# Centring the first four tiles before their transposes, and starting five FFN blocks tile by tile instead of three

## The chip, the cores and the metric

The kernel runs on one core of a Trainium2 chip. That core has a matrix engine (TensorE, PE in the profile), a vector engine (VectorE, DVE), a scalar engine (ScalarE, ACT), a general engine (GpSimd, POOL) and a sync engine (SyncE, SP) that here only issues transfers. Each works through its own list of instructions in order, and waits where an instruction needs something from another engine. The metric is the device time of one execution in microseconds (us), taken as the median of several runs.

## What is computed

The input `x` has 2048 rows (tokens) of 640 columns. Everything is in bfloat16, with sums in float32.

```
xn  = layernorm(x)                         # per row: (x - mean) / sqrt(var + 1e-5)
q, k, v = xn @ wqkv                        # 32 heads of 20 columns
phi(t) = where(t > 0, t + 1, exp(t)) + 1e-6
kv  = phi(k)^T v     per head;   z = sum over tokens of phi(k)
s   = (phi(q) kv) / (phi(q) z + 1e-6) @ wo
g   = silu(relu(xn @ w1) @ w2)             # FFN, 1728 hidden columns
out = x + s * g
```

The attention is linear: `kv` and `z` are sums over all tokens, so all of K must be known before any output row is. The FFN does not depend on the attention.

## The kernel before

The tokens are cut into 16 tiles of 128 and four groups of 512 (group j holds tiles 4j to 4j+3). Matrix products need the normalized input transposed, with the 640 columns as five chunks of 128 on the partitions; this is `xnT`. Three kinds of work use it:

- a *K block* (`K_mm`, L468) takes one tile through the K weights, 2 x 5 matmuls of 128x320;
- an *FFN block* (`H_block`, L565) takes 128 of the 1728 hidden columns for a whole group, 5 matmuls of 128x512, and ScalarE's relu then empties the PSUM bank (`H_ev`);
- a *Q block* (`Q_block`) does the same for the queries of groups 1 to 3 (those of group 0 come later).

After them come the Gram blocks `G_block` for `kv`, the FFN's second product `U_main`, and the output tiles `s_tile`. There is no planner. The order in which the calls stand in the source is the order of each engine's list, and a small bookkeeping class (`Sched`) adds the waits: an operation that reads or overwrites something waits for whoever wrote or still reads it. The PSUM banks (eight of them, `ps[0]` to `ps[7]`) are given by hand.

The first group is special, since nothing is transposed when the kernel starts. While TensorE runs filler matmuls (`fill`), the first tile is loaded, its mean and variance are found by VectorE (`LN_stats`: two statistics and one aggregate), the mean is subtracted in two parts, and the parts are transposed by TensorE (`T_first`). Tiles 1 to 3 are transposed raw (`T_raw`), copied out of PSUM, and the mean is removed afterwards: TensorE sums the 640 columns with a matrix of ones (`T_sum`, L450), and VectorE subtracts the result in place (`T_center`, L455). The division by the standard deviation is not done here for these four tiles; the readers of K and the final silu apply it as a scale. As soon as a tile is ready, the first three FFN blocks are computed for that tile alone (`H_first`, 128 columns wide), in banks 2, 3 and 4. When all four tiles are done, ScalarE empties these banks, and the list `order` (L684) goes on with K blocks of tiles 0 to 7 (`K_step`) and the FFN blocks 3 to 12 of group 0 between them. Tiles 4 to 7 are normalized by VectorE in that time (`LN_norm`, L407) and transposed by a DMA (`xnT_dma`, L463).

The transfers are issued by SP in the order of the source, each some 0.4 us after the one before; an `extra` entry holds a transfer back until a given operation is done. Only the first part of `w1` (FFN blocks 0 to 2) goes out on ScalarE's queue. `w1` is cut into three parts at the limits `W1C`; a block waits for its part alone.

Of the kernel before, what the change touches and what calls it, by code (L numbers as in the profile page):

```python
# [4 lines left out]
ALU = mybir.AluOpType  # L5
# [206 lines left out]
def bass_recurrent_scan__linear_attn_block__dense_activation_relu__prompt_kernel(  # L212
# [14 lines left out]
    P = 128  # L227
# [73 lines left out]
    mhalf = nc.alloc_sbuf_tensor("mhalf", [P, 1], f32)  # L301
    denS = nc.alloc_sbuf_tensor("denS", [P, 512], f32)
    rden = nc.alloc_sbuf_tensor("rden", [P, 512], bf)
    stats = nc.alloc_sbuf_tensor("stats", [P, T, 2, 6], f32)
    mv = nc.alloc_sbuf_tensor("mv", [P, T, 2], f32)
    rsv = nc.alloc_sbuf_tensor("rsv", [P, T], f32)
# [26 lines left out]
    def x_load(t, extra=(), E="SP"):  # L333
        sl = t % XR
        return dma(E, lambda eng: eng.dma_start(xin[:, sl, :], x2[tok(t), :]), W=[("xin", sl)], extra=extra)
# [8 lines left out]
    sc.op("POOL", lambda eng: eng.memset(ident[:], 0.0), W=[("ident",)])  # L344
    sc.op("POOL", lambda eng: eng.affine_select(out=ident[:], in_=ident[:], compare_op=ALU.not_equal,
                                                fill=1.0, base=0, pattern=[[-1, P]], channel_multiplier=1),
          R=[("ident",)], W=[("ident",)])
# [7 lines left out]
                        for _ in range(n)], W=[("ps", 0)])  # L355


    W1C = [0, 3 * P, 7 * P, FF]

    def w1_load(i, extra=()):  # L360
        w_load(w1_sb[:, :, W1C[i]:W1C[i + 1]], B_w1[:, W1C[i]:W1C[i + 1]], ("w1", i), extra)

    def w1_part(f):
        return [i for i in range(3) if W1C[i] <= P * f < W1C[i + 1]][0]

    x_load(0)
    for t in (1, 2, 3):
        x_load(t)
    dma("ACT", lambda eng: eng.dma_start(w1_sb[:, :, W1C[0]:W1C[1]],
                                         B_w1[:, W1C[0]:W1C[1]].rearrange("(c p) n -> p c n", p=P)), W=[("w1", 0)])  # L370

    def build_masks():
        sc.op("POOL", lambda eng: eng.memset(mh[:, :, :], 1.0), W=[("mh",)])
# [29 lines left out]
    def xnk(t, cs=range(C)):  # L403
        return [("xn", t, c) for c in cs]
# [6 lines left out]
            x_load(t + XR)  # L411


    def T_first(c0, c1):
        done = sc.op("DVE", lambda eng: eng.tensor_scalar(
            out=xn[:, 0, P * c0:P * c1], in0=xin[:, 0, P * c0:P * c1], scalar1=mv[:, 0, 0:1], scalar2=None,
            op0=ALU.subtract), R=[("xin", 0), ("mv", 0)], W=xnk(0, range(c0, c1)))
        b = 4 if c0 == 0 else 1
        psb = ps[b].bitcast(bf)
        sc.group("PE", [(lambda eng, c=c: eng.transpose(psb[:, P * c:P * (c + 1)], xn[:, 0, P * c:P * (c + 1)], ident[:]))  # L420
                        for c in range(c0, c1)], R=xnk(0, range(c0, c1)) + [("ident",)], W=[("ps", b)])
        out = xnT[:, c0:c1, 0:P]
        src = psb[:, P * c0:P * c1].rearrange("p (c q) -> p c q", c=c1 - c0)
        if c0 == 0:
            sc.op("ACT", lambda eng: eng.activation(out=out, in_=src, func=ACTF.Copy), R=[("ps", b)],
                  W=xtk(0, range(c0, c1)))
        else:
            sc.op("DVE", lambda eng: eng.tensor_copy(out, src), R=[("ps", b)], W=xtk(0, range(c0, c1)))
        return done


    def T_raw(t):
        psb = ps[4 + t].bitcast(bf)
        cut = 3 if t == 1 else C
        psc = ps[0].bitcast(bf)
        for c0, c1, pd, pb in [(0, cut, psb, 4 + t), (cut, C, psc, 0)]:
            if c1 > c0:
                sc.group("PE", [(lambda eng, c=c, pd=pd: eng.transpose(pd[:, P * c:P * (c + 1)],
                                                                       xin[:, t, P * c:P * (c + 1)], ident[:]))
                                for c in range(c0, c1)], R=[("xin", t), ("ident",)], W=[("ps", pb)])  # L440
        sc.op("ACT", lambda eng: eng.activation(out=xnT[:, 0:cut, tok(t)],
                                                in_=psb[:, 0:cut * P].rearrange("p (c q) -> p c q", c=cut),
                                                func=ACTF.Copy), R=[("ps", 4 + t)], W=xtk(t, range(cut)))
        if cut < C:
            sc.op("DVE", lambda eng: eng.tensor_copy(xnT[:, cut:C, tok(t)],
                                                     psc[:, cut * P:C * P].rearrange("p (c q) -> p c q", c=C - cut)),
                  R=[("ps", 0)], W=xtk(t, range(cut, C)))

    def T_sum(t):
        sc.group("PE", [(lambda eng, c=c: eng.matmul(ps[4 + t][:, 320:320 + P], lhsT=onesM[:, :], rhs=xnT[:, c, tok(t)],  # L450
                                                     start=(c == 0), stop=(c == C - 1))) for c in range(C)],
                 R=xtk(t) + [("onesM",)], W=[("ps", 4 + t)])

    def T_center(t):
        return sc.op("DVE", lambda eng: eng.scalar_tensor_tensor(  # L455
            out=xnT[:, :, tok(t)], in0=ps[4 + t][:, 320:320 + P].unsqueeze(1).to_broadcast([P, C, P]), scalar=-1.0 / D,
            in1=xnT[:, :, tok(t)], op0=ALU.mult, op1=ALU.add), R=[("ps", 4 + t)] + xtk(t), W=xtk(t))

    def xtk(t, cs=range(C)):
        return [("xnT", t, c) for c in cs]  # L460
# [93 lines left out]
    def H_mm(j, f, b, lo=0, hi=512):  # L554
        return sc.group("PE", [(lambda eng, k=k: eng.matmul(ps[b][:, lo:hi], lhsT=w1_sb[:, k, P * f:P * (f + 1)],  # L555
                                                            rhs=xnT[:, k, 512 * j + lo:512 * j + hi],
                                                            start=(k == 0), stop=(k == C - 1))) for k in range(C)],
                        R=[("w1", w1_part(f))] + [kk for q in range(lo // P, hi // P) for kk in xtk(4 * j + q)],
                        W=[("ps", b)])

    def H_ev(j, f, b):
# [9 lines left out]
    def H_halves():  # L571
        bs = [nextb(), nextb()]
        fns = []
        for jp in range(2):
            for k in range(C):
                for u in range(2):
                    fns.append(lambda eng, jp=jp, k=k, u=u: eng.matmul(  # L577
                        ps[bs[jp]][64 * u:64 * (u + 1), :], lhsT=w1_sb[:, k, NF * P:FF],
                        rhs=xnT[:, k, schunk(2 * jp + u)], start=(k == 0), stop=(k == C - 1)))
        sc.group("PE", fns, R=[("w1", 2)] + [kk for q in range(16) for kk in xtk(q)], W=[("ps", b) for b in bs])  # L580
# [5 lines left out]
    def H_first(t, f):  # L586
        H_mm(0, f, (2, 3, 4)[f], P * t, P * t + P)
        if t == 3:
            H_ev(0, f, (2, 3, 4)[f])
# [24 lines left out]
    T_sum(3)  # L614
    T_center(3)
    H_first(1, 1)
    H_first(1, 2)
    for t in (2, 3):
        for f in range(3):
            H_first(t, f)  # L620
    LN_stats(1)
    LN_stats(2)
    LN_stats(3)

    def z_split():
        sc.op("POOL", lambda eng: eng.tensor_copy(zhl[:, 0, :], zacc[:, :]), R=[("zacc",)], W=[("zhi",)])
# [31 lines left out]
    def K_step(t):  # L658
        b = (0, 6)[t % 2]
        K_mm(t, b)  # L660
        K_exp(t, b)
        K_relu(t, b)
        if t == 0:
            LN_stats(4)
        if t == 1:
            LN_norm(4)
            xnT_dma(4)
            LN_stats(5)
# [332 lines left out]
```

## Time and profile before

| | us |
|---|---|
| median of 3 runs | 223.0 (222.99 to 223.22) |
| the profiled execution | 223.15 |
| its span, from the first to the last instruction | 221.4 |
| TensorE busy in the span | 215.8 |
| TensorE's share of the chain that ended last | 95% |
| first K block starts | 11.48 |
| first transposed tile starts on TensorE | 4.93 |

The span is what the profile shows; the 1.75 us beside it lie before the first and after the last instruction. In the profile's rows, an instruction is named by its line in the source, its engine, its operation and the program's names of what it writes and reads. `reg` and `psT` are the big buffers in SBUF and PSUM; the matmuls of FFN blocks are L555, of K blocks L472, of Q blocks L540. A row of the timeline starts with its start and its duration in us, and ends with the idle time before it and what ended that, in square brackets. Matmuls overlap, so the duration of one is longer than the step from one to the next.

### The profile page before, as it was taken

To read this page: it belongs to the slowest core of one execution; us is meant where nothing else is said; L and a number is where in the kernel's file an instruction comes from. 1 tells how busy PE (TensorE), PEld (TensorE's weight loads), DVE (VectorE), ACT (ScalarE), POOL (GpSimd) and SP (SyncE) were. 2 spreads that over 40 slices of the span, in tenths; PEclk is the share of its full clock that TensorE was granted. 3 is DMA by queue.
4 is the path that set the end of the run, shared out by engine and by line. 5 is a ranking of instruction groups with operands and counts; after the bars stand their busy time and mean duration, and the time that the engine had idled before them with its cause. 6 is when DMAs were issued, how large, how long until landed. Compare 5 with 4: busy or idle time off the path is not lost.

```text
span 221.4 us, 3528 instructions
## 1 busy us (share of the span) xinstructions
PE 215.8 (97%) x1463; PEld 133.9 (60%) x1474; DVE 114.6 (52%) x193; ACT 86.1 (39%) x138; POOL 43.7 (20%) x66
## 2 busy tenths in 40 slices
PE   7999999999999999999999999999999999999994
PEld 2865554455545554444467778767767776776672
DVE  2687845889687999996710006603322222314063
ACT  2368665567656656555322114641021102110300
POOL 4053101259222998700000000000000000000001
PEclk9999999999999999999999999999999999999999
DMA  6899581211012105800059969369110101000002
GB/s 190 242 357 250 131 234 41 59 30 33 0 30 59 33 0 104 170 12 3 0 178 365 272 178 353 93 201 322 62 59 3 61 30 33 30 31 33 30 30 89
DMA packets 28156, 24.51 MB, mean 111 GB/s; under 512 B 11796, under 2 KB 27500, under 8 KB 28140
## 3 DMA queue, kind: packets, MB, share of 16 engines
q1 hardware_dynamic: 27484, 23.79, 36.7%
q10 hardware_dynamic: 656, 0.49, 0.8%
q8 instruction: 11, 0.18, 0.4%
q14 instruction: 5, 0.04, 0.1%
HBM read 15.75 MB, written 5.24 MB: 95 GB/s over the span
## 4 chain that ended last, share of the span: by engine, by line
PE 95%; DVE 1%; DMA 1%; issue 0%; ACT 0%
PE psT L841 26%; PE psT L555 25%; PE psT L472 10%; PE psT L786 10%; PE psT L540 10%; PE psT L887 10%; DMA reg<-in_A_x_dram 1%; PE psT L857 1%; PE psT L577 1%; PE psT L797 1%; PE psT L808 1%; PE psT L645 1%; PE psT L450 1%; DVE reg L902 0%; DVE stats L392 0%
## 5 line engine op out<-in xcount | busy, mean ns | idle before, releaser
L555 PE MATMUL psT<-reg 128*128 128x512 bf16 (+1 forms) x295 | 59.8, 346 | 0.7 <-issue 0.2
L841 PE MATMUL psT<-reg,hT 128*128 128x320 bf16 x416 | 60.1, 299 | 0.0
L841 PEld LDWEIGHTS psT<-reg,hT 128*128 128x128 bf16 x416 | 40.4, 98 | 16.4 <-issue 1.1
L555 PEld LDWEIGHTS psT<-reg 128*128 128x128 bf16 x305 | 27.3, 98 | 26.8 <-issue 0.4
L909 DVE TENSOR_TENSOR reg<-psT,reg 128x640 bf16<-128x640 f32 x15 | 12.4, 825 | 54.0 <-PE psT L887 53.9
L562 ACT ACTIVATE hT<-psT 128x512 bf16<-128x512 f32 x52 | 30.9, 598 | 18.2 <-PE psT L555 18.1
L875 ACT ACTIVATE reg<-psT 128x640 bf16<-128x640 f32 (+1 forms) x13 | 8.4, 661 | 44.3 <-PE psT L841 24.9
L894 POOL TENSOR_TENSOR reg<-reg 128x320 bf16<-128x320 bf16 x1 | 0.8, 788 | 124.6 <-DVE reg L902 124.6
L540 PE MATMUL psT<-reg 128*128 128x512 bf16 x99 | 24.6, 379 | 0.1
L472 PE MATMUL psT<-reg 128*128 128x320 bf16 x160 | 24.2, 299 | 0.0
L481 POOL TENSOR_TENSOR zacc<-zacc,reg 128x640 f32<-128x640 f32 x16 | 23.7, 1484 | 1.9 <-DVE reg L515 1.0
L887 PE MATMUL psT<-reg,pqT 128*128 128x320 bf16 (+2 forms) x165 | 24.0, 295 | 0.0
L786 PE MATMUL psT<-reg 128*128 128x320 bf16 x160 | 21.9, 299 | 0.0
L472 PEld LDWEIGHTS psT<-reg 128*128 128x128 bf16 x160 | 15.6, 98 | 8.2
L887 PEld LDWEIGHTS psT<-reg,pqT 128*128 128x128 bf16 x165 | 15.9, 98 | 6.0
L786 PEld LDWEIGHTS psT<-reg 128*128 128x128 bf16 x160 | 15.7, 98 | 6.2
L550 DVE SCALAR_TENSOR_TENSOR pqT<-er 128x512 bf16<-128x512 bf16 x20 | 17.1, 853 | 0.7
L540 PEld LDWEIGHTS psT<-reg 128*128 128x128 bf16 x100 | 9.7, 98 | 11.7 <-DVE er L548 0.6
L392 DVE BATCH_NORM_STATS2 stats<-reg 128x6 f32<-128x320 bf16 x32 | 14.0, 478 | 3.4 <-DMA reg<-in_A_x_dram 3.4
L547 ACT ACTIVATE er<-psT 128x512 bf16<-128x512 f32 x20 | 12.0, 598 | 8.9 <-PE psT L540 8.1
L548 DVE TENSOR_SCALAR er<-psT 128x512 bf16<-128x512 f32 x20 | 13.6, 679 | 3.1 <-ACT er L547 3.1
L515 DVE TENSOR_TENSOR reg<-ek 128x640 bf16<-128x640 bf16 x16 | 13.5, 843 | 1.5 <-ACT ek L506 1.0
(66 smaller groups left out, 134.6 us busy)
## 6 DMA issues: line engine op xcount, KB each, us to landing
reg<-in_A_x_dram SPq DMA_DIRECT2D x16, 160.0 KB, 4.1
rscr<-rden SPq DMA_DIRECT2D x4, 640.0 KB, 10.7
reg<-rscr SPq DMA_DIRECT2D x5, 512.0 KB, 6.1
reg<-in_A_x_dram SPq DMA_DIRECT2D x4, 640.0 KB, 6.2
out_dram<-reg SPq DMA_DIRECT2D x15, 160.0 KB, 1.8
reg<-in_A_wqkv_dram SPq DMA_DIRECT2D x2, 800.0 KB, 6.9
reg<-in_B_w_dram SPq DMA_DIRECT2D x1, 1120.0 KB, 5.9
reg<-in_B_w_dram SPq DMA_DIRECT2D x1, 1040.0 KB, 7.6
```

The lines of the kernel that those rows point to most:

```text
L392: sc.op("DVE", lambda eng, a=a: eng.bn_stats(stats[:, t, a, :], xv[:, HN * a:HN * (a + 1)]), R=[("xin", t % XR)], W=[("stats", t, a)])
L472: fns.append(lambda eng, a=a, k=k: eng.matmul(ps[b + a][:, 0:HN], lhsT=xnT[:, k, tok(t)], rhs=wqk[:, k, D + HN * a:D + HN * (a + 1)], star ...
L481: sc.op("POOL", lambda eng: eng.tensor_tensor(out=zacc[:, :], in0=zacc[:, :], in1=pk[:, t, :], op=ALU.add), R=[("zacc",), ("pk", t)], W=[( ...
L515: sc.op("DVE", lambda eng: eng.tensor_tensor(out=pk[:, t, :], in0=e_, in1=r_, op=ALU.add), R=[("ek_e", es), ("ek_r", es)], W=[("pk", t)])
L540: sc.group("PE", [(lambda eng, k=k: eng.matmul(ps[b], lhsT=wqk[:, k, P * f:P * (f + 1)], rhs=rhs(k), start=(k == 0), stop=(k == C - 1))) f ...
L548: sc.op("DVE", lambda eng: eng.tensor_scalar(out=r_, in0=ps[b], scalar1=0.0, scalar2=1e-6, op0=ALU.max, op1=ALU.add), R=[("ps", b), ("er_e ...
L550: sc.op("DVE", lambda eng: eng.scalar_tensor_tensor(out=pqT[:, f, schunk(j)], in0=e_, scalar=1.0, in1=r_, op0=ALU.min, op1=ALU.add), R=[(" ...
L555: return sc.group("PE", [(lambda eng, k=k: eng.matmul(ps[b][:, lo:hi], lhsT=w1_sb[:, k, P * f:P * (f + 1)], rhs=xnT[:, k, 512 * j + lo:512 ...
L562: sc.op("ACT", lambda eng: eng.activation(out=hT[:, f, schunk(j)], in_=ps[b], func=ACTF.Relu), R=[("ps", b)], W=[("hT", j, f)])
L786: fns.append(lambda eng, t=t, a=a: eng.matmul(ps[b + a][:, 0:HN], lhsT=xn[:, t, P * k:P * (k + 1)], rhs=pk[:, t, HN * a:HN * (a + 1)], sta ...
L841: sc.group("PE", [(lambda eng, f=f, n=n: eng.matmul(ps[b + n][:, 0:HN], lhsT=hT[:, f, tok(t)], rhs=w2_sb[:, f, HN * n:HN * (n + 1)], start ...
L887: sc.group("PE", [(lambda eng, c=c, pb=pb, lo=lo, hi=hi: eng.matmul(ps[pb][:, 0:hi - lo], lhsT=pqT[:, c, tok(t)], rhs=wf[:, c, lo:hi], sta ...
```

## The change

Each of the first four tiles is now centred by VectorE before it is transposed (`center`, then `T_pe`, then `T_copy`), and the sums on TensorE are gone. Tiles 0 and 1 take their mean from `LN_stats`; tiles 2 and 3 take it from a ScalarE copy that also accumulates its output (`T_mean`). Its main output goes to a scratch area. Five FFN blocks instead of three are computed tile by tile, in banks 2 to 6, and `order` starts at block 5. `w1` has four parts; the second (blocks 3 and 4) is issued between the x loads of tiles 2 and 3. The first part, still on ScalarE's queue, now waits for the memset of `ident` on POOL. There are nine fillers instead of eight, both copies of tile 0 are ScalarE's, statistics of tiles 1 to 3 come earlier on VectorE, and in `K_step(0)` the statistics and the normalization of tile 4 move ahead.

```diff
-    W1C = [0, 3 * P, 7 * P, FF]
+    W1C = [0, 3 * P, 5 * P, 9 * P, FF]
...
     x_load(0)
-    for t in (1, 2, 3):
-        x_load(t)
+    x_load(1)
     dma("ACT", lambda eng: eng.dma_start(w1_sb[:, :, W1C[0]:W1C[1]],
...
+        extra=[began])
+    x_load(2)
+    w1_load(1)
+    x_load(3)
...
+    def T_mean(t):
+        sc.op("ACT", lambda eng: eng.activation(out=ek[:, 0, 0, :], in_=xin[:, t, :], func=ACTF.Copy, scale=1.0 / D,
+                                                accum_out=mean[:, t:t + 1]),
+              R=[("xin", t)], W=[("mean", t), ("ek_e", 0)])
+    def center(t, c0, c1):
+        mk, m = (("mv", t), mv[:, t, 0:1]) if t < 2 else (("mean", t), mean[:, t:t + 1])
+        return sc.op("DVE", lambda eng: eng.tensor_scalar(
+            out=xn[:, t, P * c0:P * c1], in0=xin[:, t, P * c0:P * c1], scalar1=m, scalar2=None,
+            op0=ALU.subtract), R=[("xin", t), mk], W=xnk(t, range(c0, c1)))
+    def T_pe(t, c0, c1, b):
+        psb = ps[b].bitcast(bf)
+        sc.group("PE", [(lambda eng, c=c: eng.transpose(psb[:, P * c:P * (c + 1)], xn[:, t, P * c:P * (c + 1)], ident[:]))
+                        for c in range(c0, c1)], R=xnk(t, range(c0, c1)) + [("ident",)], W=[("ps", b)])
...
-    fill(8)
+    HF = [2, 3, 4, 5, 6]
+    def H_first(t, fs=range(5), ks=range(C)):
+        for f in fs:
+            H_mm(0, f, HF[f], P * t, P * t + P, ks)
+            if t == 3:
+                H_ev(0, f, HF[f])
+    fill(9)
     LN_stats(0)
-    T_first(0, 2)
-    w_load(wqk[:, :, D:2 * D], A_wqkv[:, D:2 * D], ("wk",), [T_first(2, 5)])
+    center(0, 0, 2)
+    T_pe(0, 0, 2, 7)
+    held = center(0, 2, 5)
+    T_pe(0, 2, 5, 1)
+    T_copy("ACT", 0, 0, 2, 7)
+    T_copy("ACT", 0, 2, 5, 1)
+    w_load(wqk[:, :, D:2 * D], A_wqkv[:, D:2 * D], ("wk",), [held])
     fill(1, 384)
-    T_raw(1)
-    H_first(0, 0)
-    H_first(0, 1)
-    T_sum(1)
-    held = [T_center(1)]
-    w1_load(1, held)
+    H_first(0, (0, 1, 2), (0, 1))
+    H_first(0, (0, 1, 2), (2, 3, 4))
+    LN_stats(1)
+    center(1, 0, 2)
+    T_pe(1, 0, 2, 7)
+    held = center(1, 2, 5)
+    T_pe(1, 2, 5, 1)
+    T_mean(2)
+    T_copy("ACT", 1, 0, 2, 7)
+    T_copy("DVE", 1, 2, 5, 1)
+    w1_load(2, [held])
     x_load(4)
     x_load(5)
-    w1_load(2)
+    w1_load(3)
     x_load(6)
     x_load(7)
     w_load(wqk[:, :, 0:D], A_wqkv[:, 0:D], ("wq",))
-    T_raw(2)
-    H_first(0, 2)
-    T_raw(3)
-    T_sum(2)
-    T_center(2)
-    H_first(1, 0)
-    T_sum(3)
-    T_center(3)
-    H_first(1, 1)
-    H_first(1, 2)
-    for t in (2, 3):
-        for f in range(3):
-            H_first(t, f)
-    LN_stats(1)
+    H_first(0, (3, 4))
+    T_mean(3)
+    center(2, 0, C)
+    H_first(1, (0, 1))
+    T_pe(2, 0, C, 7)
+    T_copy("ACT", 2, 0, C, 7)
+    center(3, 0, C)
+    H_first(1, (2, 3, 4))
+    T_pe(3, 0, C, 1)
+    T_copy("ACT", 3, 0, C, 1)
     LN_stats(2)
     LN_stats(3)
+    H_first(2)
+    H_first(3, (4, 0, 1, 2, 3))
...
-    order = [("K", 0), ("K", 1), 3, ("K", 2), 4, ("K", 3), 5, 6, 7, ("K", 4), 8, ("K", 5), 9, 10, ("K", 6), 11, ("K", 7), 12]
+    order = [("K", 0), ("K", 1), 5, ("K", 2), 6, ("K", 3), 7, 8, ("K", 4), 9, ("K", 5), 10, ("K", 6), 11, ("K", 7), 12]
...
-            H_block(0, a, (5, 2, 3, 4)[(a - 3) % 4])
-        if a == 4:
+            H_block(0, a, (2, 3, 4, 5)[(a - 5) % 4])
+        if a == 6:
...
-        if a == 6:
+        if a == 8:
...
-    ring[0] = 1
+    ring[0] = 0
```

More of the change, by code (lines that the diff above doesn't have):

```diff
@@ L303, in bass_recurrent_scan__linear_attn_block__dense_activation_relu__prompt_kernel @@
     rden = nc.alloc_sbuf_tensor("rden", [P, 512], bf)
+    mean = nc.alloc_sbuf_tensor("mean", [P, 4], f32)
     stats = nc.alloc_sbuf_tensor("stats", [P, T, 2, 6], f32)
@@ L343, in bass_recurrent_scan__linear_attn_block__dense_activation_relu__prompt_kernel @@
     sc.op("POOL", lambda eng: eng.memset(onesM[:, :], 1.0), W=[("onesM",)])
-    sc.op("POOL", lambda eng: eng.memset(ident[:], 0.0), W=[("ident",)])
+    began = sc.op("POOL", lambda eng: eng.memset(ident[:], 0.0), W=[("ident",)])
     sc.op("POOL", lambda eng: eng.affine_select(out=ident[:], in_=ident[:], compare_op=ALU.not_equal,
@@ L411, in LN_norm @@
             x_load(t + XR)
[L414 to L418, printed above, removed]
-        psb = ps[b].bitcast(bf)
[L420 to L424, printed above, removed]
+    def T_mean(t):
+        sc.op("ACT", lambda eng: eng.activation(out=ek[:, 0, 0, :], in_=xin[:, t, :], func=ACTF.Copy, scale=1.0 / D,
+                                                accum_out=mean[:, t:t + 1]),
+              R=[("xin", t)], W=[("mean", t), ("ek_e", 0)])
@@ L425, in T_first, with T_copy @@
+    def T_copy(E, t, c0, c1, b):
+        out = xnT[:, c0:c1, tok(t)]
+        src = ps[b].bitcast(bf)[:, P * c0:P * c1].rearrange("p (c q) -> p c q", c=c1 - c0)
+        if E == "ACT":
             sc.op("ACT", lambda eng: eng.activation(out=out, in_=src, func=ACTF.Copy), R=[("ps", b)],
-                  W=xtk(0, range(c0, c1)))
+                  W=xtk(t, range(c0, c1)))
         else:
-            sc.op("DVE", lambda eng: eng.tensor_copy(out, src), R=[("ps", b)], W=xtk(0, range(c0, c1)))
-        return done
@@ L432, in T_raw @@
[L432 to L457, printed above, removed]
+            sc.op("DVE", lambda eng: eng.tensor_copy(out, src), R=[("ps", b)], W=xtk(t, range(c0, c1)))
@@ L552, in Q_block, with H_mm @@
               R=[("er_e", es), ("er_r", es)], W=[("pqT", j, f)])
-    def H_mm(j, f, b, lo=0, hi=512):
+    def H_mm(j, f, b, lo=0, hi=512, ks=range(C)):
         return sc.group("PE", [(lambda eng, k=k: eng.matmul(ps[b][:, lo:hi], lhsT=w1_sb[:, k, P * f:P * (f + 1)],
                                                             rhs=xnT[:, k, 512 * j + lo:512 * j + hi],
-                                                            start=(k == 0), stop=(k == C - 1))) for k in range(C)],
-                        R=[("w1", w1_part(f))] + [kk for q in range(lo // P, hi // P) for kk in xtk(4 * j + q)],
+                                                            start=(k == 0), stop=(k == C - 1))) for k in ks],
+                        R=[("w1", w1_part(f))] + [kk for q in range(lo // P, hi // P) for kk in xtk(4 * j + q, ks)],
                         W=[("ps", b)])
@@ L579, in H_halves @@
                         rhs=xnT[:, k, schunk(2 * jp + u)], start=(k == 0), stop=(k == C - 1)))
-        sc.group("PE", fns, R=[("w1", 2)] + [kk for q in range(16) for kk in xtk(q)], W=[("ps", b) for b in bs])
+        sc.group("PE", fns, R=[("w1", NP - 1)] + [kk for q in range(16) for kk in xtk(q)], W=[("ps", b) for b in bs])
         for jp in range(2):
@@ L661, in K_step @@
         K_exp(t, b)
+        if t == 0:
+            LN_stats(4)
         K_relu(t, b)
         if t == 0:
-            LN_stats(4)
-        if t == 1:
             LN_norm(4)
             xnT_dma(4)
+        if t == 1:
             LN_stats(5)
```

10 lines of the change are left out of this document (4 added, 6 removed).

## The prediction

> **What bounds the kernel now.** I read the page's busy shares first, then the chain that ended last, then busy time by stage, then TensorE's rows up to the first K block.
>
> ```profile
> PE 215.8 (97%) x1463; PEld 133.9 (60%) x1474; DVE 114.6 (52%) x193; ACT 86.1 (39%) x138; POOL 43.7 (20%) x66
> PE 95%; DVE 1%; DMA 1%; issue 0%; ACT 0%
> 0.00:4.90 4.90, 3.57 (x8) 1.02 (x8) 1.41 (x5) 1.28 (x1) 1.70 (x10) 1.00 0.60 164
> 4.90:11.40 6.50, 6.23 (x95) 5.60 (x96) 4.19 (x10) 2.45 (x5) 0.63 (x2) 1.00 0.85 262
> 11.40:34.00 22.60, 22.44 (x136) 13.19 (x137) 16.53 (x45) 16.31 (x27) 6.08 (x14) 1.00 0.84 239
> ```
>
> TensorE holds 95% of the chain: from 4.93 us on, the end moves with TensorE's work plus its waits. (The window rows give stage, its length, then busy us of PE, PEld, DVE, ACT, POOL, clock, DMA share, GB/s.) No other engine is full from 4.9 to 34 us, the stretch that the change rewrites. Its TensorE rows:
>
> ```profile
> 0.82 3.57 PE L354 MATMUL psT<-const-bfloat16-1.0 128*128 128x512 bf16 x8 [0.82 <-PEq L986]
> 4.93 0.73 PE L420 MATMUL psT<-ident,reg 128*128 128x128 bf16 x5 [0.54 <-DVE reg L415]
> 5.45 0.53 PE L354 MATMUL psT<-const-bfloat16-1.0 128*128 128x384 bf16 x1
> 5.77 0.51 PE L438 MATMUL psT<-ident,reg 128*128 128x128 bf16 x5
> ...
> 6.85 0.44 PE L450 MATMUL psT<-reg,onesM 128*128 128x128 bf16 x5
> ...
> 8.36 0.45 PE L450 MATMUL psT<-reg,onesM 128*128 128x128 bf16 x5 [0.24 <-ACT reg L441]
> ...
> 9.24 2.40 PE L555 MATMUL psT<-reg 128*128 128x128 bf16 x40
> 11.48 1.79 PE L472 MATMUL psT<-reg 128*128 128x320 bf16 x12
> ```
>
> The first K block starts at 11.48 us. The 40 matmuls start at 9.24 and the K block follows at 11.48, so a 128-wide matmul costs (11.48 - 9.24)/40 = 0.056 us. Before it TensorE issues 95 of them plus a filler. The chain's own pieces give the 512-wide price:
>
> ```profile
> 11.64 2.72 PE psT L472 x20
> 16.80 1.08 PE psT L555 x5
> ```
>
> A block of five 512-wide matmuls is 1.08 us.
>
> **The change on TensorE.** Removed: three times five column sums (L450), 15 x 0.056 = 0.84 us; and FFN blocks 3 and 4 of group 0 in 512-wide form, 2 x 1.08 = 2.16 us, which stood between the K blocks. Added: the same blocks as 2 x 4 x 5 = 40 matmuls of 128, 40 x 0.056 = 2.24 us, ahead of the first K block. So the matmul work falls by 0.76 us, and all later work is 2.16 us closer to the first K block. The gain is 2.16 us less the delay of that block: with it at 11.48 + 2.16 = 13.64 us nothing is won. The ninth filler costs (3.57 - 0.63)/7 = 0.42 us (0.63 is one filler's whole duration, shown in no further step) and lies in the 0.54 us wait ahead of 4.93; without that cover it would cost 0.42.
>
> When can the first K block start? Three paths reach it. Their durations:
>
> ```profile
> 3.42 0.89 DVE L392 BATCH_NORM_STATS2 stats<-reg 128x6 f32<-128x320 bf16 x2 [3.42 <-DMA reg<-in_A_x_dram]
> 4.34 0.21 DVE L394 BATCH_NORM_AGGREGATE mv<-stats 128x2 f32<-128x12 f32 x1
> 4.59 0.52 DVE L415 TENSOR_SCALAR reg<-reg,mv 128x256 bf16<-128x256 bf16 x2
> 5.36 0.38 ACT L425 ACTIVATE reg<-psT 128x256 bf16<-128x256 bf16 x1 [2.81 <-PE psT L420]
> 5.70 0.36 DVE L428 COPY reg<-psT 128x384 bf16<-128x384 bf16 x1 [0.59 <-PE psT L420]
> 6.21 0.49 ACT L441 ACTIVATE reg<-psT 128x384 bf16<-128x384 bf16 x1 [0.46 <-PE psT L438]
> 7.32 0.82 DVE L455 SCALAR_TENSOR_TENSOR reg<-psT,reg 128x640 bf16<-128x640 f32 x1 [0.71 <-PE psT L450]
> 7.60 1.30 ACT L441 ACTIVATE reg<-psT 128x640 bf16<-128x640 bf16 x2 [0.90 <-PE psT L438]
> L407 DVE TENSOR_SCALAR reg<-reg,mv,rsy 128x640 bf16<-128x640 bf16 x9 | 3.8, 443 | 2.6 <-POOL rsy L398 2.6
> ```
>
> Path 1, TensorE itself. Tile 0's two copies now both run on ScalarE: 5.36 to 5.74 and, from 5.70, 0.49 us to 6.19. Six matmuls need the first copy and run from 5.80; nine need the second, 6.24 to 6.74. Tile 1's five transposes end at 7.02. Behind them stand 10 (blocks 3, 4 of tile 0), 25 and 5 (tile 1, tile 2's transposes), 5 (tile 3's) and 50 matmuls: 95 x 0.056 = 5.3 us, so 12.3.
>
> Path 2, tile 1. VectorE is free at 5.11. Statistics take 3.42 to 4.55, so 1.13; the two centrings 0.52: 5.11 to 6.8. Transposes end at 7.02, VectorE's copy runs from about 7.25 to 7.65, and 85 matmuls (all that stand behind tile 0's blocks) take 4.75: 12.4. That needs tile 1's x by 5.1.
>
> Path 3, the new w1 part: its landing, 0.05, and the 95 matmuls.
>
> ```profile
> 0.78 0.45 ACTq L369 DMA_DIRECT2D reg<-in_B_w_dram  x1
> 0.79 1.82 SPq L335 DMA_DIRECT2D reg<-in_A_x_dram  x4
> 0.93 0.20 POOL L344 MEMSET ident<- 128x128 bf16 x1
> reg<-in_B_w_dram ACTq DMA_DIRECT2D x1, 480.0 KB, 4.4
> reg<-in_A_wqkv_dram SPq DMA_DIRECT2D x1, 800.0 KB, 4.7
> DMA to landing us min/median/max: 2.6/4.3/4.4
> 4.50:5.00 0.50, 0.07 (x1) 0.07 (x2) 0.47 (x3) 0.00 (x0) 0.32 (x1) 1.00 1.10 396
> 6.00:6.50 0.50, 0.50 (x12) 0.50 (x10) 0.23 (x2) 0.29 (x1) 0.00 (x0) 1.00 0.65 69
> ```
>
> (Fifth row: the K weights, issued at 5.1; sixth: the first four x loads.) SP issues one load in 1.82/4 = 0.46 us, so tile 1's x, issued at 1.25, lands at 5.65 before, tile 2's at 1.7 + 4.4 = 6.1, w1's first part at 0.78 + 4.4 = 5.2. Now that part waits for POOL's memset (ends 1.13), so it is issued at about 1.2 and lands near 5.6, behind tile 1's x instead of ahead of it; the table load behind it on ScalarE is needed only at 5.36. When tile 2's x is in, 960 KB have moved, as before: 6.1 again. The new part's 320 KB follow it on SP's queue, in rows of 512 bytes that no row here shows: at the best rate (396 GB/s) 0.83 us, and at 60% of it, since a row of 512 is two thirds of the first part's 768, about 1.4. It lands between 6.95 and 7.5. I take 7.25, nearer the fast end, since the queue is then continuously full, unlike at 6 us before (69 GB/s) when the K weights had only just been asked for. Path 3 gives 7.25 + 0.05 + 5.3 = 12.6; ends 12.3 and 12.85.
>
> Path 3 is latest: first K block at 12.6, gain 2.16 - 1.12 = 1.04 us.
>
> **What I cost at nothing.** ScalarE's two means are new. Their kind with an accumulator is not in the trace; the 640-wide copies (0.65 each) are nearest, I take 0.8 with ends 0.65 and 1.3. The first stands in ScalarE's queue ahead of tile 1's copy: x of tile 2 at 6.1, ScalarE free at 6.19, so 7.0 against 7.2 when the transposes are ready. At 1.3 it delays that copy by 0.3, and TensorE is by then still in tile 0's blocks (7.3 to 7.85). The second waits for tile 3's x, which now lands behind the new part, 0.45 later: 7.7. Mean 8.5, centring 0.45: 9.0, while TensorE reaches tile 3's transposes near 9.5. Behind that mean stands tile 2's copy; it has slack until x lands at about 8.2. VectorE loses three corrections (L455, 0.82 each) and gains a whole tile's centring twice; its statistics of tiles 2 and 3 move ahead. The K weights are issued by the same centring at 5.1 and landed at 5.1 + 4.7 = 9.8; with up to 1.4 us for the new part in front, 11.2, over 1 us before need. The held w1 part, x loads 4 to 7 and the Q weights follow tile 1's centring (6.8) instead of its correction (7.32 + 0.82 = 8.14 before), so all are issued earlier.
>
> Next the K stage, where two FFN blocks less stand between K3 and K7.
>
> ```profile
> 14.66 0.87 DVE L392 BATCH_NORM_STATS2 stats<-reg 128x6 f32<-128x320 bf16 x2
> 24.77 0.45 DVE L407 TENSOR_SCALAR reg<-reg,mv,rsy 128x640 bf16<-128x640 bf16 x1 [0.46 <-POOL rsy L398]
> 25.62 1.21 SPq L463 DMA_TRANSPOSE reg<-reg  x1
> reg<-reg SPq DMA_TRANSPOSE x16, 2.6
> 30.70 1.52 PE L472 MATMUL psT<-reg 128*128 128x320 bf16 x10
> ```
>
> K7 comes 1.04 earlier, 29.7. Its transposed tile was issued at 25.62 and lands about 2.6 later, 28.2; VectorE's chain before it holds the same operations, so 28.2 to 28.5, 1.2 us in hand. Moving statistics 4 ahead of the relu of K0 costs nothing: tile 4's x is asked for 1.3 us earlier than before, where these statistics ran at 14.66 without a wait, and K0's exp, which the relu needs, starts only when K0 ends, 12.6 + 1.36 = 14.0. Bank 6, now used by block 4, is read out first of the five; K1 needs it 1.4 us after K0 starts. From group 1 on the order is unchanged and only shifts.
>
> **The sum.** Profiled execution 223.15 us (span 221.4), 0.15 above the median of the runs, 223.0. 223.15 - 1.04 = 222.1 profiled, and **222.0 as a median**.
>
> **Rivals.** *A: the first w1 part still goes ahead of tile 1's x.* Then x lands at 5.65 to 5.75, path 2 is 0.6 later, the new part lands past its slow end, and the first K block comes near 13.1 and the time is 222.5. For it: before, x1 to x3 all landed behind that part although issued at about the same time. Against it: the part is now issued 0.4 us later. One row for and the delay against: 0.15. [...]
>
> *B: slower, by the new part's landing.* It is ahead of tile 3's x on SP's queue and TensorE waits for it in order. At the rates of 6 us (69 GB/s) for only part of the 320 KB it would land past 8.3, and from there on the change loses: 8.3 + 5.35 = 13.64. At 9.0 the time is 223.7. For it: such a dip stands in the profile; against it: it stood where the queue had run empty.
>
> *C: full matmul rate comes later.* Fillers cost 0.42 per 512 columns against 1.08/5 = 0.216 later, so the rate doubles on the way. If TensorE's new small waits at 5.77 and 6.14 put that off by another stretch as long as the fillers' (3.57 us), 32 matmuls of 128 fit in instead of 64; 32 x 0.056 = 1.8 us, of which 0.4 falls into waits: 223.4. Against it: the ninth filler closes most of the 0.54 gap. [...]
>
> *D: nothing won*, because the K stage gives it back: tile 7's transpose landing at 29.6 or later plus a wait at K6 takes 1 us: 223.0. Slack of 1.2 speaks against it.
>
> **How the numbers follow.** Main case 0.65 (own range 221.5 to 222.3, from paths at 12.3 to 12.85 with 0.1 for the runs' spread), A 0.15, B 0.10, C 0.06, D 0.04. About 0.2%, 0.45 us, is what can be told from no change. Faster: the main case and most of A, 0.78; same: C, D and the rest of A, 0.12; slower: B, 0.10. The range reaches from 221.4 (all paths at 12.3 and x 0 landing earlier without the weights beside it, worth up to 0.33 since nine fillers end at 0.82 + 9 x 0.42 = 4.6) to 223.4, which takes in A, C and D.
>
> **What would show it.** After: no sums on TensorE; first K block near 12.6, with the wait before it on the new w1 part at 7.0 to 7.3; tile 1's statistics starting at once after tile 0's centring, near 5.1 (at 5.7, A); K and FFN blocks without waits up to 32 us, and everything behind shifted by 1.04. I am wrong if TensorE waits past 8.3 for weights, if matmuls of 128 still step by 0.11 (twice 0.056) at 6.5, or if a wait opens at K2, K6 or K7.

## The result, and the profile after

The changed kernel takes 222.2 us (median of 6 runs, 221.93 to 222.63) against 223.07 for the kernel before (6 runs, 222.91 to 223.22). The ratio is 0.9961, with a 95% interval of 0.9949 to 0.9974. In a second set, taken beside experiment 1, it took 222.53 (10 runs, 221.89 to 223.69) against 223.06 (33 runs, 222.77 to 223.42), ratio 0.9976 (0.9961 to 0.9991). It is faster by 0.2 to 0.4%, and its runs are spread wider than those before.

The profiled execution took 222.63 us, the longest of its six, with a span of 220.8. First the busy shares and the chain that ended last, by engine; then TensorE's timeline (start, duration, instruction, and in brackets the idle time before it with what ended it):

```profile
PE 215.1 (97%) x1479; PEld 134.1 (61%) x1490; DVE 113.4 (51%) x193; ACT 87.8 (40%) x143; POOL 43.8 (20%) x66
PE 95%; DMA 2%; DVE 1%; issue 0%; SPq 0%
```

```profile
4.62 0.57 PE L435 MATMUL psT<-ident,reg 128*128 128x128 bf16 x5
5.02 0.33 PE L355 MATMUL psT<-const-bfloat16-1.0 128*128 128x384 bf16 x1
6.06 1.00 PE L543 MATMUL psT<-reg 128*128 128x128 bf16 x15 [0.72 <-DMA reg<-in_B_w_dram]
7.21 0.57 PE L435 MATMUL psT<-ident,reg 128*128 128x128 bf16 x5 [0.15 <-DVE reg L429]
7.62 1.35 PE L543 MATMUL psT<-reg 128*128 128x128 bf16 x20
8.81 0.44 PE L435 MATMUL psT<-ident,reg 128*128 128x128 bf16 x5
9.09 1.00 PE L543 MATMUL psT<-reg 128*128 128x128 bf16 x15
9.93 0.44 PE L435 MATMUL psT<-ident,reg 128*128 128x128 bf16 x5
10.20 2.96 PE L543 MATMUL psT<-reg 128*128 128x128 bf16 x50
13.00 2.88 PE L460 MATMUL psT<-reg 128*128 128x320 bf16 x20
```

The sums are gone, and TensorE starts 0.31 us earlier on tile 0 (4.62 against 4.93). Then it waits for the first w1 part (0.72) and for tile 1's centring (0.15). From 7.6 us on, up to the first K block, it does not wait any more. The first K block starts at 13.00 instead of 11.48, and the span behind it is 220.8 - 13.00 = 207.8 us instead of 221.4 - 11.48 = 209.9: the two 512-wide blocks, 2.16 us, have moved ahead of it. Net, the span lost 0.6 us.

The chain that ended last passes through the transfer of tile 1's x, VectorE's work on it and its transposes (start, duration, what):

```profile
1.25 4.43 DMA reg<-in_A_x_dram
5.71 0.90 DVE stats L397 x2
7.21 0.57 PE psT L435 x5
```

VectorE's and ScalarE's rows of the same stretch show why tile 1 is late, and what the means cost:

```profile
3.11 0.89 DVE L397 BATCH_NORM_STATS2 stats<-reg 128x6 f32<-128x320 bf16 x2 [3.11 <-DMA reg<-in_A_x_dram]
5.71 0.89 DVE L397 BATCH_NORM_STATS2 stats<-reg 128x6 f32<-128x320 bf16 x2 [0.92 <-DMA reg<-in_A_x_dram]
6.87 0.52 DVE L429 TENSOR_SCALAR reg<-reg,mv 128x256 bf16<-128x256 bf16 x2
8.10 0.38 DVE L429 TENSOR_SCALAR reg<-reg,mean 128x640 bf16<-128x640 bf16 x1
6.41 0.74 ACT L421 ACTIVATE ek<-reg 128x640 bf16<-128x640 bf16 x1 [0.70 <-DMA reg<-in_A_x_dram]
7.05 0.19 ACT L421 ACTIVATION_READ_ACCUMULATOR ek<-reg 128x1 f32 x1
```

VectorE is done with tile 0 at 4.8 and sits idle for 0.92 us until tile 1's x lands just before 5.71. A mean is two instructions on ScalarE, 0.74 us and a read of the accumulator of 0.19, 0.83 from start to end.

### The profile page after: what moved, and what is told of

Read it like the earlier page. It is cut to its first block, busy times and chain, and to the rows that moved or that the text cites. A ratio compares the mean times of both kernels' runs of the same rounds, so it can differ in the third digit from the quotient of the medians.

```text
span 220.8 us, 3565 instructions
## 1 busy us (share of the span) xinstructions
PE 215.1 (97%) x1479; PEld 134.1 (61%) x1490; DVE 113.4 (51%) x193; ACT 87.8 (40%) x143; POOL 43.8 (20%) x66
## 4 chain that ended last, share of the span: by engine, by line
PE 95%; DMA 2%; DVE 1%; issue 0%; SPq 0%
PE psT L841 26%; PE psT L543 25%; PE psT L786 10%; PE psT L460 10%; PE psT L528 10%; PE psT L887 10%; DMA reg<-in_A_x_dram 2%; PE psT L857 1%; PE psT L565 1%; PE psT L797 1%; PE psT L808 1%; PE psT L644 1%; PE psT L435 1%; DVE reg L902 0%; DVE stats L397 0%
## 5 line engine op out<-in xcount | busy, mean ns | idle before, releaser
L543 PEld LDWEIGHTS psT<-reg 128*128 128x128 bf16 x335 | 28.5, 98 | 26.6 <-ACT reg L442 1.0
L909 DVE TENSOR_TENSOR reg<-psT,reg 128x640 bf16<-128x640 f32 x15 | 12.4, 825 | 54.0 <-PE psT L887 54.0
L460 PEld LDWEIGHTS psT<-reg 128*128 128x128 bf16 x160 | 15.5, 98 | 8.3 <-ACT ek L481 0.3
L786 PEld LDWEIGHTS psT<-reg 128*128 128x128 bf16 x160 | 15.7, 98 | 6.2
L528 PEld LDWEIGHTS psT<-reg 128*128 128x128 bf16 x100 | 9.7, 98 | 11.7 <-DVE er L536 0.6
```

The source lines that it names most:

```text
L460: fns.append(lambda eng, a=a, k=k: eng.matmul(ps[b + a][:, 0:HN], lhsT=xnT[:, k, tok(t)], rhs=wqk[:, k, D + HN * a:D + HN * (a + 1)], star ...
L528: sc.group("PE", [(lambda eng, k=k: eng.matmul(ps[b], lhsT=wqk[:, k, P * f:P * (f + 1)], rhs=rhs(k), start=(k == 0), stop=(k == C - 1))) f ...
L786: fns.append(lambda eng, t=t, a=a: eng.matmul(ps[b + a][:, 0:HN], lhsT=xn[:, t, P * k:P * (k + 1)], rhs=pk[:, t, HN * a:HN * (a + 1)], sta ...
```

## The experiments

The span behind the first K block depends only on how many FFN blocks are taken tile by tile before it, so for a given number of them the start of that block tells the time of a profiled execution. (The landings of tile 1's x and of the new w1 part, the K block and the span are those of the profiled execution; the median is that of n runs.) Beside every set the kernel before took 223.05 to 223.13. The changed kernel itself took 222.20 and 222.53 in its two sets, so medians that differ by no more than that are not told apart here.

| version | x of tile 1 | new w1 part | first K block | span | median us (range, n) |
|---|---|---|---|---|---|
| before | 5.65 | - | 11.48 | 221.4 | 223.07 (222.91 to 223.22, 6) |
| changed | 5.68 | 7.35 | 13.00 | 220.8 | 222.20 (221.93 to 222.63, 6) |
| 1 changed again | 5.26 | 7.14 | 12.58 | 220.4 | 222.53 (221.89 to 223.69, 10) |
| 2 weights on SP | 3.56 | 7.94 | 13.30 | 221.1 | 223.21 (222.62 to 224.87, 12) |
| 3 three blocks | 5.66 | - | 11.71 | 221.7 | 223.20 (222.77 to 223.56, 11) |
| 4 five blocks, raw | 5.57 | 7.41 | 13.49 | 221.3 | 223.28 (222.89 to 224.47, 12) |
| 5 statistics 4 back | 5.80 | 7.08 | 13.11 | 220.9 | 222.54 (222.22 to 224.08, 12) |
| 6 x 1 on ScalarE | 3.87 | 7.20 | 12.58 | 220.3 | 222.32 (221.99 to 224.43, 12) |
| 7 means by VectorE | 5.30 | 7.29 | 13.85 | 221.6 | 223.64 (223.07 to 224.77, 12) |
| 8 as 2, four fillers | 3.57 | 7.15 | 12.51 | 220.3 | 222.95 (221.78 to 223.36, 12) |
| 9 two fillers | 5.41 | 7.36 | 12.82 | 220.6 | 222.54 (222.15 to 223.55, 12) |
| 10 x 1 on ScalarE, held | 3.79 | 7.31 | 12.67 | 220.4 | 222.16 (221.70 to 224.98, 12) |
| 11 four first fillers | 5.17 | 7.15 | 14.27 | 222.1 | 223.75 (222.93 to 225.19, 12) |
| 12 as 10, four fillers | 3.56 | 6.84 | 12.62 | 220.5 | 222.17 (221.76 to 222.65, 6) |

Behind the first K block 207.7 to 207.9 us follow in every version with five blocks, and 209.9 to 210.0 in the two with three.

**1. The changed kernel again.** No edit; a second profile.

> The changed kernel as it is, a second profile. In its first profile the first K block started at 13.00 us and tile 1's x landed at 5.68, beside the first w1 part. Theory (tile 1's x sets the first K block): in every profile the first K block starts 7.3 us after that x lands, and the span is 207.8 us longer than its start. If x lands at 5.2 this time, the block starts at 12.5. Rival (the new w1 part sets it): the block starts 5.35 us after that part lands, whatever tile 1's x does. Time near 222.2.

```profile
5.29 0.89 DVE L397 BATCH_NORM_STATS2 stats<-reg 128x6 f32<-128x320 bf16 x2 [0.45 <-DMA reg<-in_A_x_dram]
6.81 0.56 PE L435 MATMUL psT<-ident,reg 128*128 128x128 bf16 x5
12.58 2.88 PE L460 MATMUL psT<-reg 128*128 128x320 bf16 x20
```

(VectorE's, then TensorE's timeline of this run.) Tile 1's x landed 0.42 us earlier and the first K block started 0.42 us earlier, 7.32 us after it both times. The rival's distance from the new w1 part was 5.65 and 5.44, not constant. But the equal distance is partly luck. Here TensorE goes to tile 1's transposes at 6.81 without a wait, and the chain that ended last comes from the first w1 part (issued at 1.16, landed at 5.74) and tile 0's matmuls behind it. So this execution, 222.1 us, is already at the limit of tile 0's matmuls; a still earlier x would gain little by itself.

**2. The first w1 part on SP's queue.**

```diff
-    dma("ACT", lambda eng: eng.dma_start(w1_sb[:, :, W1C[0]:W1C[1]], ...
+    w1_load(0)
     x_load(2)
```

> One change to the changed kernel: the first w1 part is issued by SP between the x of tiles 1 and 2, not by ScalarE, so no second queue runs beside tile 1's x. Theory (tile 1's x is slowed by the second queue and sets the first K block): x of tile 1 lands near 4, its statistics start at once after tile 0's centring (4.8), its transposes are ready when tile 0's first 15 matmuls end, and the next limit is the new w1 part (7.4): first K block at 12.7, 0.3 us better than 222.2, so 221.9. Rival (SP's issue time matters more): each later load goes out 0.46 us later, the new part lands at 7.8, the first K block starts at 13.15 and the time is 222.3 to 222.4.

```profile
6.68 1.00 PE L541 MATMUL psT<-reg 128*128 128x128 bf16 x15 [1.32 <-DMA reg<-in_B_w_dram]
7.98 0.11 PEld L541 LDWEIGHTS psT<-reg 128*128 128x128 bf16 x2 [0.20 <-DMA reg<-in_B_w_dram]
```

(TensorE's matmuls, then its weight loads.) Tile 1's x landed at 3.56 instead of 5.26 to 5.68, so the second queue beside it did slow it. The gain was eaten on the other side: the first w1 part landed at 6.55 instead of 5.74 to 5.93, TensorE waited 1.32 us, and the new part landed at 7.94 with the K block 5.36 us behind it. The rival was right in this profile, and its time of 222.4 was still too low: the profiled execution took 222.95, and the runs have a group of four above 224. The ratio to the kernel before is 1.0019 (0.9997 to 1.0040).

**3. The centring without the two further blocks.** Three blocks tile by tile, w1 in three parts, the old list of K and FFN blocks.

```diff
-    W1C = [0, 3 * P, 5 * P, 9 * P, FF]
+    W1C = [0, 3 * P, 7 * P, FF]
-    H_first(0, (3, 4))
-    H_first(1, (2, 3, 4))
+    H_first(1, (2,))
-    H_first(3, (4, 0, 1, 2, 3))
+    H_first(3)
...
```

> The centring part of the change alone: three FFN blocks tile by tile as before, three w1 parts, the list of K and FFN blocks of before; centring, means by ScalarE, fillers and the held first part stay. Theory (the sums' 0.84 us alone only turn into waits for tile 1, 2 and 3, since their chain of statistics, centring, transposes and copies is longer than the raw one): first K block at 11.4 to 11.75, no better than 11.48; 223.0 to 223.3. Rival (the removed sums are the gain): 222.2 to 222.4, first K block at 10.7.

```profile
8.22 0.73 PE L542 MATMUL psT<-reg 128*128 128x128 bf16 x10 [0.45 <-DVE reg L444]
10.02 1.85 PE L542 MATMUL psT<-reg 128*128 128x128 bf16 x30 [0.24 <-ACT reg L441]
11.71 2.88 PE L459 MATMUL psT<-reg 128*128 128x320 bf16 x20
```

(TensorE's timeline.) The sums' 0.84 us are gone and nothing is gained: ratio 1.0004 (0.9995 to 1.0012). Their place is taken by waits for tile 1's copy (0.45) and tile 2's (0.24), and by tile 1's transposes, which start at 7.19. In this profile two things keep them until then. The full matmul rate comes later: tile 0's fifteen matmuls take 1.46 us, against 1.00 and 1.09 in the two profiles of the changed kernel. And tile 1's x landed at 5.66, so that its centring starts at 6.85, 0.34 us ahead of the transposes as in the changed kernel (6.87 and 7.21).

**4. Five blocks with the raw transposes and the sums.** The kernel before, with blocks 3 and 4 taken tile by tile behind the third correction.

```diff
+    w1_load(1)
...
+    for t in (0, 1):
+        for f in (3, 4):
+            H_first(t, f)
     for t in (2, 3):
-        for f in range(3):
+        for f in (4, 3, 0, 1, 2):
...
-        b = (0, 6)[t % 2]
+        b = (6, 0)[t % 2]
```

> The block part of the change alone: the kernel before, with raw transposes and sums, but five FFN blocks tile by tile (blocks 3 and 4 in banks 5 and 1, the first K block in banks 6 and 7) and the further w1 part asked for behind tile 3's x. Theory (there is hardly any wait before the first K block to be filled: 0.24 us): the 40 narrow matmuls cost 2.24 us and save 2.16, first K block at 13.7, 223.0 to 223.2. Rival (five blocks alone fill waits): first K block at 13.1 or earlier, 222.4.

The first K block started at 13.49, 2.01 us later than before for 2.16 us saved behind it, and the ratio is 1.0016 (1.0002 to 1.0030), with four of twelve runs from 223.87 to 224.47. (It is 0.2 earlier than forecast mainly because TensorE started on tile 0 at 4.75 instead of 4.93: that x had landed at 3.22 instead of 3.40.) So neither part of the change gains alone. Centring ahead makes TensorE's work shorter and its waits longer; the two further blocks give it work to do in those waits.

**5. Tile 4's statistics back behind the relu.**

```diff
         K_exp(t, b)
-        if t == 0:
-            LN_stats(4)
         K_relu(t, b)
         if t == 0:
-            LN_norm(4)
-            xnT_dma(4)
+            LN_stats(4)
         if t == 1:
+            LN_norm(4)
+            xnT_dma(4)
             LN_stats(5)
```

> One change to the changed kernel: in the first K steps, the statistics and the normalization of tile 4 go back to where they were before the change (behind the relus of K0 and K1). Theory (the move only buys slack in the K stage): tile 7's transpose is issued 0.9 us later, near 26.6, and lands near 28.9, still before K7 at 29.6 to 30.0, so the time stays at 222.2 to 222.5, with a longer upper tail at most. Rival (without the move the K stage gives the gain back, rival D of the prediction): a wait ahead of K6 or K7, 222.8 to 223.2.

```profile
27.24 1.21 SPq L451 DMA_TRANSPOSE reg<-reg  x1
30.19 1.52 PE L460 MATMUL psT<-reg 128*128 128x320 bf16 x10
```

Tile 7's transpose (SP's row) is issued at 27.24 instead of 26.01, later than the 26.6 that I expected, and K7 (TensorE's row) still starts without a wait. The median is that of the changed kernel beside experiment 1. Three runs lie near 224, and the ratio to the kernel before is 0.9987 (0.9966 to 1.0009). The move buys slack that the profiled execution did not need; whether the three long runs needed it stays open, since none was profiled. Tile 1's x landed at 5.80 here, and the first K block followed 7.31 us behind it, with that transfer on the chain again.

**6. Tile 1's x on ScalarE's queue, the first w1 part on SP's.**

```diff
-    x_load(1)
-    dma("ACT", lambda eng: eng.dma_start(w1_sb[:, :, W1C[0]:W1C[1]], ...
+    x_load(1, E="ACT")
+    w1_load(0)
```

> One change to the changed kernel: ScalarE issues tile 1's x at once, and SP issues the first w1 part right behind tile 0's x. Theory (tile 1's x, between 5.26 and 5.68 in two profiles of the changed kernel, sets the first K block when it is late, and its variation makes much of the spread): that x lands before 4.5, VectorE works on tile 1 from 4.85 on, TensorE goes straight from tile 0's 15 matmuls to tile 1's transposes, the limits are the w1 parts (5.9 and 7.15), the first K block starts at 12.5 in every profile, median 222.0. Rival (x beside x slows tile 0's x, and the first w1 part comes later behind it): tile 0's x at 3.4, first part at 6.3, first K block at 13, 222.5 or more.

```profile
3.71 0.89 DVE L395 BATCH_NORM_STATS2 stats<-reg 128x6 f32<-128x320 bf16 x2 [3.71 <-DMA reg<-in_A_x_dram]
5.22 0.57 PE L433 MATMUL psT<-ident,reg 128*128 128x128 bf16 x5 [0.39 <-DVE reg L427]
```

Both held in part. Tile 1's x landed at 3.87 and the K block started at 12.58, but tile 0's x was slowed from 3.1 to 3.7 by the second one beside it, and TensorE started on tile 0 at 5.22 instead of 4.62. The median, 222.32, cannot be told from the changed kernel's, and two of the twelve runs are above 223.6.

**7. The means of tiles 2 and 3 by VectorE.**

```diff
-    T_mean(2)
...
-    T_mean(3)
+    LN_stats(2)
     center(2, 0, C)
...
+    LN_stats(3)
     center(3, 0, C)
```

> One change to the changed kernel: the means of tiles 2 and 3 come from VectorE's statistics, right ahead of their centring, instead of ScalarE's accumulating copy. Theory (with the means on VectorE its chain of 1.13 us of statistics and 0.4 of centring per tile is longer than TensorE's work between the tiles, 0.84 to 1.1): tile 2's transposes wait until about 9.3, tile 3's until 10.95, first K block at 14.0, 1.4 us later than in the changed kernel; 223.6 to 223.8, slower than before. Rival (VectorE has room, since three corrections of 0.82 went): first K block by 13, 222.2 to 222.6.

```profile
9.31 0.45 PE L435 MATMUL psT<-ident,reg 128*128 128x128 bf16 x5 [0.69 <-DVE reg L429]
10.77 0.45 PE L435 MATMUL psT<-ident,reg 128*128 128x128 bf16 x5 [0.17 <-DVE reg L429]
13.85 0.43 PE L460 MATMUL psT<-reg 128*128 128x320 bf16 x2
```

As forecast: TensorE waits for tile 2 and tile 3, and the kernel is slower than before, ratio 1.0027 (1.0010 to 1.0045). Without ScalarE's two means nothing is left of the gain.

**8. Experiment 2 with the wait filled.**

```diff
-    fill(1, 384)
+    fill(4, 384)
```

> The kernel that issues the first w1 part on SP, with four 384-wide fillers instead of one behind tile 0's transposes, in the 1.3 us in which TensorE waits for that part. That kernel's runs fell into two groups, 222.6 to 223.4 (8 runs) and 224.2 to 224.9 (4 runs). [...] Rival (the upper group is transfers that land late): the two groups stay, a third of the runs above 224.

All twelve runs lie below 223.4, where experiment 2 had four of twelve above 224. Two groups remain inside, four runs from 221.78 to 222.15 and eight from 222.66 to 223.36; in the profile, of one of those four, the first w1 part landed at 5.73, not 6.55. So the rival's third of the runs above 224 did not come. Long runs that come from the wait (rival C of the prediction) would be gone like this, but that is not shown: none against four of twelve, on two different chips, can be chance. What is left of the spread fits a part that lands at either of two times.

**9. One more filler in the changed kernel.** `fill(2, 384)` in place of `fill(1, 384)`.

> One change to the changed kernel: two 384-wide fillers instead of one behind tile 0's transposes, in the wait for the first w1 part. Theory (some executions of the changed kernel, those above 223 us, have the full matmul rate late, because the waits near 5.5 and 7 us leave a stretch too idle): no run above 223.2, median 222.1 to 222.3. Rival (the long executions come from late transfers): about one run in six stays above 223.2.

Inconclusive: two runs of twelve are above 223.2 (223.21 and 223.55) and the median is 222.54, not lower.

**10. Tile 1's x on ScalarE's queue, held by the memset, and two fillers.**

```diff
-    x_load(1)
-    dma("ACT", lambda eng: eng.dma_start(w1_sb[:, :, W1C[0]:W1C[1]], ...
+    x_load(1, extra=[began], E="ACT")
+    w1_load(0)
...
-    fill(1, 384)
+    fill(2, 384)
```

> The changed kernel with tile 1's x on ScalarE's queue, held by the memset like the first w1 part was, the first w1 part on SP's queue behind tile 0's x, and two 384-wide fillers behind tile 0's transposes. Theory (tile 1's x, then the w1 parts limit): tile 0's x at 3.1, tile 1's below 4.5, first part at 5.3 to 5.7, new part at 7.1, first K block at 12.4 to 12.5 in every profile; median 221.9 to 222.0, no run above 223. Rival (the first part on SP lands late in part of the runs, as it did at 6.55 in one profile of the kernel with SP issuing it): a second group near 222.8.

```profile
6.88 0.44 PE L433 MATMUL psT<-ident,reg 128*128 128x128 bf16 x5
7.35 1.12 PEld L541 LDWEIGHTS psT<-reg 128*128 128x128 bf16 x20 [0.20 <-DMA reg<-in_B_w_dram]
12.67 2.06 PE L458 MATMUL psT<-reg 128*128 128x320 bf16 x14
```

Tile 0's x lands at 3.1 again, tile 1's at 3.79, and its transposes follow tile 0's matmuls without a wait. Now the new w1 part (7.31) is the limit, with the K block 5.36 us behind it, the distance that the prediction's third path had as 5.35. The forecast of 12.4 to 12.5 was missed, with the first w1 part landing at 5.91 and not by 5.7. Ten runs lie between 221.70 and 222.43, but two are at 223.85 and 224.98, where the forecast had none above 223.

**11. Four fillers at the start instead of nine.** `fill(4)` in place of `fill(9)`.

> One change to the changed kernel: four fillers instead of nine at the start. They end at 2.5 us, 2.1 us before tile 0's transposes, and delay nothing in either kernel. [...] Rival (the rate depends on the time since the start alone): no change, 222.2 to 222.5.

```profile
0.83 1.86 PE L355 MATMUL psT<-const-bfloat16-1.0 128*128 128x512 bf16 x4 [0.83 <-PEq L986]
4.67 0.73 PE L435 MATMUL psT<-ident,reg 128*128 128x128 bf16 x5 [1.98 <-DVE reg L429]
5.86 1.76 PE L543 MATMUL psT<-reg 128*128 128x128 bf16 x15
7.94 2.30 PE L543 MATMUL psT<-reg 128*128 128x128 bf16 x20
10.36 1.00 PE L543 MATMUL psT<-reg 128*128 128x128 bf16 x15
14.27 0.43 PE L460 MATMUL psT<-reg 128*128 128x320 bf16 x2
```

The rival, no change, is refuted. Tile 0's transposes start at the same time, but fifteen matmuls take 1.76 us at 5.86 and 1.00 at 10.36: the rate doubled only near 10. Twenty from 7.94 on and the five transposes behind them (from 10.08 to 10.36) give the steps: (10.08 - 7.94)/20 = 0.107 us, then 0.28/5 = 0.056. The median is 223.75, 0.3% above before (ratio 1.0026, 1.0006 to 1.0045). Five fillers that fill nothing but idle time are worth 1.2 to 1.6 us here (223.75 against 222.53 and 222.20).

**12. Experiment 10 with four fillers in the wait.**

> The kernel with tile 1's x on ScalarE's queue, with four 384-wide fillers instead of two behind tile 0's transposes. Ten of that kernel's runs lay between 221.7 and 222.5, two at 223.85 and 224.98. Theory (the two long runs come from the wait of some 0.5 to 0.7 us for the first w1 part, which leaves a stretch too idle for the full rate): no run above 223, at the price of up to 0.4 us where the rate is still low and the fillers outlast the wait; median 222.1 to 222.4. Rival (late transfers or something else): one or two runs in twelve above 223.5 again.

Six runs, all from 221.76 to 222.65, ratio 0.9960 (0.9948 to 0.9972). That agrees with the theory, but six runs without a long one do not show that there are none. In the profile TensorE shows no wait from 0.82 us on, and tile 0's matmuls start at 6.13, behind the fillers, although the first w1 part had landed at 5.41. So by the chain it is TensorE's own work, and no transfer, that sets this K block's start of 12.62. As measured, this version and the changed kernel cannot be told apart by their medians.

## Why the prediction was right, point by point

It forecast 222.0 (221.4 to 223.4) and faster; 222.2 was measured, a gain of 0.87 us where 1.04 was forecast, and 0.53 beside experiment 1. What the gain consists of is as predicted: work moved ahead of the first K block, less that block's delay. Which path sets the delay is not. The prediction had the new w1 part last, at 12.6. In the first profile tile 1's x came last, and the block started at 13.00. In the second, tile 0's matmuls behind the first w1 part came last, at 12.58, while the new w1 part, landed at 7.14, would have let it start at 12.50. That 12.58 is so near 12.6 is in part luck. The profiled executions, 222.63 and 222.10 us, lie on both sides of the first median; which path came last in the other runs is not known.

**The matmul count.** 2.16 us of work moved ahead of the first K block: the span behind it fell by 2.1. Right. So the gain of a profiled execution with five blocks is 13.64 less the K block's start, for example 13.64 - 13.00 = 0.64 and 13.64 - 12.58 = 1.06 in the two profiles of the changed kernel.

**The ninth filler** at nothing: right, though with hardly any cover left. Tile 0's x landed 0.3 us earlier (3.08 against 3.40), and still its transposes start no later than with four fillers (4.62 and 4.67 against 4.67 in experiment 11).

**Path 1, tile 0's matmuls from 5.80.** They started at 6.06 and 5.87, since the first w1 part landed at 5.93 and 5.74, not 5.6. In the second profile this was the path that came last, with the K block at 12.58 instead of 12.3.

**Path 2, tile 1.** This is the step that was off. It "needs tile 1's x by 5.1", and the held weights were to land "behind tile 1's x instead of ahead of it". They did land behind it, at 5.93 and 5.74, but that x came no sooner for it in the first profile, 5.68 against 5.65 before, and at 5.26 in the second. The held part was still issued first (1.16 against 1.25), and in none of the seven profiles that issue it so did tile 1's x land by 5.1: it landed between 5.17 and 5.80. In the first profile that is the landing of rival A, though the part did not go ahead of the x, and its K block, 13.1, came too: 13.00, with tile 1's statistics at 5.71, the prediction's own sign of A. The time of 222.5 that it gave for A compares with 222.63 in that execution. With the weights on the same queue, behind it, that x landed at 3.56 (experiment 2), so the transfer on the other queue cost it 1.7 to 2.1 us against the two profiles of the changed kernel. I gave rival A too small a chance, 0.15.

**Path 3, the new w1 part at 7.25** with ends 6.95 and 7.5: 7.35 and 7.14, and 5.36 us to the K block where this part comes last (experiments 2, 8 and 10). So its landing and its distance were right, with two errors that cancel in part: tile 2's x landed at 6.39 and 6.18, not 6.1, and the new part 0.96 us behind it, not 1.15. That this path comes last was wrong in both profiles of the changed kernel; TensorE never waited there for the new part. Rival B, a landing past 8.3, did not occur; 7.94 was the latest.

**ScalarE's means** at 0.8 with ends 0.65 and 1.3: 0.83. Right, and experiment 7 shows that VectorE could not have taken them for nothing.

**The K stage** at nothing: no wait ahead of any K block in the profiles (rival D); tile 7's transpose was issued at 26.01 and 25.60, 25.6 to 25.9 by the forecast of its landing.

**Rival C, the full rate late.** It was not the common case, but experiment 11 shows that the rate can come late, and the price, 1.2 to 1.6 us; and in experiment 8 a group of long runs was missing after a wait was filled. With four fillers at the start matmuls of 128 still stepped by 0.107 us up to 10.08 and by 0.056 from there on. In the first profile of the changed kernel the full rate was there by 5.02, where the 384-wide filler takes 0.33 us (0.53 in experiment 11), and in the second from shortly after 5.87, with 0.52 for that filler and 1.09 for the fifteen matmuls behind it. How much work the rate needs ahead of it is not shown; the 3.57 us of the prediction were my estimate from the fillers' row. Whether all long runs come from it stays open. None of them was profiled; experiments 9 and 10 still had two each after one more filler, and experiment 4 has a long group in spite of TensorE's rows being those of before up to 9 us.

## What to carry to other kernels

Taking work off the engine that is the bound gains only where that engine is not made to wait in its place: here the shorter preparation and the work that fills its longer waits were worth nothing apart and 0.2 to 0.4% together. When a kernel's tail is fixed, find the one event behind which the span does not change; each variant is then the latest of a few paths to that event. When several paths end within 0.1 to 0.4 us of each other, a total can come out right by another path than the one named, so look at the chain. A transfer on a second queue slowed the one beside it here: a short one that was needed first landed at 5.17 to 5.80 beside the long one, at 3.56 ahead of it on the same queue, and at 3.56 to 3.87 alone on the other queue. No version gained clearly by that; in experiments 2, 8 and 10 the new weights came last in its place.

## What had not been expected of the hardware

- In experiment 11 matmuls ran at half rate until about 10.08 us, although TensorE had no long wait from 4.67 us on: after one idle stretch of 1.98 us the full rate came 4 to 5 us later than in the two profiles of the changed kernel (shortly after 5.87, and by 5.02).
- A ScalarE copy of 128x640 from SBUF with accumulation is two instructions, 0.74 and 0.19 us, against 0.70 for a copy of the same width from PSUM.
- Rows of 512 bytes were moved at nearly the price of longer ones: the new part of 320 KB landed 0.96 us behind tile 2's x in the first profile (6.39 to 7.35), 340 GB/s, and tile 3's x, 160 KB in rows of 1280 bytes, 0.45 us behind that (7.80), 364 GB/s. So the slowdown to 60%, an estimate of the prediction, did not come.
